# Attention of a sixth pair in chunks of 64 tokens, a new order of steps, and 24 matmuls whose result nobody reads

## The chip, the cores and the metric

The kernel runs on one core of a Trainium2 chip. Its engines work side by side, each through its own list of instructions in order, and wait for one another by semaphores: TensorE (PE) multiplies, VectorE (DVE) and ScalarE (ACT) read PE's results from PSUM and do elementwise work, GpSimd (POOL) does elementwise work in SBUF, and SyncE (SP) issues most of the DMA transfers. The metric is the time of one execution on the device in microseconds (us); smaller is better. Before the change the median of six runs is 210.73 us (210.42 to 212.49).

## The reference

Two layers follow each other. The first is causal attention with a decay per head, written in blocks of 64 tokens with a running state; the second is layer norm, a two-layer MLP with ReLU, and a residual. Batch 4, 8 heads, 768 tokens, head size 64, model width 512, hidden width 2048.

```python
for b in range(nb):                       # blocks of 64 tokens
    intra = (qb @ kb.T * Dmask) @ vb      # Dmask[i, j] = lam ** (i - j) for i >= j
    inter = (qb * lam_pow) @ kv_state
    out[:, :, sl] = intra + inter
    kv_state = lam_block * kv_state + (kb * rev_pow).T @ vb
x = out, heads side by side               # 4 x 768 x 512
xn = (x - mean) / sqrt(var + 1e-6) * g_ln
result = x + relu(xn @ w_ch1) @ w_ch2
```

## The kernel before

The 4 x 768 tokens are cut into 12 windows of 256 tokens ("pairs" u = 0 to 11, a pair being two tiles of 128 tokens), four batches for each third of the sequence. The attention of a pair is computed by one of two methods. Pairs below `LB` (L60, six of them) use chunks of 128 tokens: two rounds of scores with 128 columns (`scores`, L273), four masks, and 64 small matmuls to apply them to the values (`av`, L419). Pairs from `LB` on use chunks of 64 tokens: one round of 32 scores matmuls with 64 columns (`scores64`, L353), two masks, and 32 matmuls (`av64`, L406), but a state after every chunk, so that VectorE makes two sums of 128x256 more (`Smid`, L388) and GpSimd two conversions more (`Sm`, L396). Each small matmul uses a quarter of the array and four run at once. `inter` (L432) adds what the state gives, `kv` (L307) or `kv64` (L372) makes the new state's terms.

The method also decides how the inputs are laid out. Below `LB`, `fill` (L76) loads k, q and v each with one transfer of 512 KB whose runs hold two tokens (512 bytes); from `LB` on (L80) with two transfers of 256 KB whose runs hold one token (256 bytes). `in_k_one`, `in_q_one` and `in_v` scale and convert a loaded pair to bf16 on the engine that the call names; `transpose_dma` (L257) transposes q (second argument 1) or k (0) by a DMA from SP's queue into `kqT`.

The MLP of a pair is a group g of 16 "units" of PE work. For groups 2 and 3, eight units of the first layer (`m1`, L530, 8 matmuls of 256 columns each, evicted by ScalarE at L533) and eight of the second (`m2`, L666, 4 matmuls of 512 columns). From group 4 on the second layer is computed with seven products instead of eight (`m2w`, L565), for which VectorE forms sums of weights (`w_sums`) and of hidden activations (`m2s[g].sums`).

The order of everything is written out by hand: a list of calls in which `units(n)` issues the next n units and the other calls issue attention steps, loads, conversions and transposes between them. The order in which calls stand is the order in every engine's list. Attention steps of pairs below `LB` stand alone (`s1`, `s2`, `s3`, `s4`); where the 64-token method begins, two pairs are interleaved by `X1` and `X2`, and from then on by `X`:

```python
def X1(u):                    def X2(u):
    av(u - 1, range(NP))          scores64(u)
    inter(u - 1, 0)               inter(u - 1, 1)
    kv64(u)                       mask64(u, 0)
    states64(u, 0)                norm(u - 1, 0)
    states64(u, 1)                norm(u - 1, 1)
                                  mask64(u, 1)
```

`X(u)` is the same in one piece. `inter` ends with `reader` (L443), a small copy from PSUM after which PE may write the second half into the same banks; up to pair 4 it runs on VectorE, later on ScalarE.

PSUM's eight banks carry names: `sc` (two), `po0`, `po1`, and `mm` (four), which `m1`, `m2`, `m2w`, `kv` and `kv64` take in turn. A bank is given again in the order in which its earlier holders are finished with in the list. `kin`, `qin`, `vin` and `kq` have three buffers each.

At the start, the norm weight arrives as one row and is spread over 128 partitions by a matmul with ones (`g_all`, L180, in the bank `po1`).

Of the kernel before, what the change touches and what calls it, by code (L numbers as in the profile page):

```python
# [7 lines left out]
F32 = mybir.dt.float32  # L8
# [9 lines left out]
def kernel(  # L18
# [11 lines left out]
    nc = tc.nc  # L30
# [26 lines left out]
    half = [slice(0, 64), slice(64, 128)]  # L57
    XB = 3
    X_PE = (2, 3, 4)
    LB = 6  # L60

    def mm_tile(shape, dtype, name):
        return ps.tile(shape, dtype, tag="mm", bufs=4, name=name)
# [29 lines left out]
    def load_in(u, name, eng):  # L93
        got = qkv_in[u][name]
        fill(got, name, u, slice(0, H), eng)
        qkv_in[u][name] = got.rearrange("p h (j d) -> p h j d", j=2)
# [28 lines left out]
    g_row = const.tile([128, DM], F32)  # L125
    g_one = wk.tile([1, DM], F32, tag="xc", name="g_one")
    nc.scalar.dma_start(g_one, moe_g_ln[None, :])


    ident = const.tile([128, 128], BF16)  # L130
# [20 lines left out]
    def make_keep64():  # L151
        for dst, base in ((keep64, 0), (keep64_b, D)):
            nc.gpsimd.memset(dst, 1.0)
            nc.gpsimd.affine_select(
                out=dst, in_=dst, compare_op=ALU.is_ge, fill=0.0,
                base=base, pattern=[[1, D]], channel_multiplier=-1,
            )
        nc.vector.tensor_copy(keep64[half[1]], keep64_b[half[1]])
# [18 lines left out]
    ones = const.tile([1, 128], F32)  # L177
    nc.vector.memset(ones, 1.0)
    g_all = ps.tile([128, DM], F32, tag="po1", name="g_all")
    nc.tensor.matmul(g_all, lhsT=ones, rhs=g_one, start=True, stop=True)  # L180

    lnlam = const.tile([128, H], F32)
# [15 lines left out]
    def open_window(u):  # L198
        kq = wk.tile([128, 2, NP, 2, 2, D], BF16, tag="kq", bufs=3, name="kq")
        vb = wk.tile([128, H, 2, D], BF16, tag="vb", bufs=4, name="vb")  # L200
        st[u] = dict(kq=kq, vb=vb)
        if u < XB:
            st[u]["kqT"] = wk.tile([128, 2, NP, 2, 128], BF16, tag="kqT", bufs=3, name="kqT")
# [25 lines left out]
    def in_k_one(u, eng, j):  # L229
        src = qkv_in[u]["k"].rearrange("p (a e) j d -> p a e j d", e=2)  # L230
        (eng.copy if eng is nc.scalar else eng.tensor_copy)(part(0, st[u]["kq"], ALL)[:, :, :, j], src[:, :, :, j])

    def in_q_one(u, eng, j):
        src = qkv_in[u]["q"].rearrange("p (a e) j d -> p a e j d", e=2)
        lq = (lam_q[:, :, j] if u < LB else lam_p[:, 0, :]).rearrange("p (a e) -> p a e", e=2)
        eng.tensor_tensor(part(1, st[u]["kq"], ALL)[:, :, :, j], src[:, :, :, j],  # L236
                          lq[:, :, :, None].to_broadcast([128, NP, 2, D]), op=ALU.mult)

    def in_v(u, eng, hs=ALL):
        n = hs.stop - hs.start  # L240
        lv = lam_v[:, hs, :, None] if u < LB else lam_p[:, 1, hs, None, None]
        eng.tensor_tensor(st[u]["vb"][:, hs], qkv_in[u]["v"][:, hs], lv.to_broadcast([128, n, 2, D]), op=ALU.mult)  # L242
# [453 lines left out]
    def store(u):  # L696
        for j in range(2):
            nc.sync.dma_start(rows_of(u)[j], o_of[u][half[j]])
# [82 lines left out]
    def w_sums(c, n):  # L781
        v = w2[c].rearrange("p (k e) d -> p k e d", e=2)
        w = DM // 2
        b11, b12, b21, b22 = v[:, :, 0, 0:w], v[:, :, 0, w:], v[:, :, 1, 0:w], v[:, :, 1, w:]
        t1, t2, t3, t4 = (wt[c][:, :, i] for i in range(4))
        if n == 0:
            nc.vector.tensor_tensor(t1, b12, b11, op=ALU.subtract)
            nc.vector.tensor_tensor(t3, b12, b22, op=ALU.add)
        else:
            nc.vector.tensor_tensor(t2, b11, t3, op=ALU.subtract)  # L790
            nc.vector.tensor_tensor(t4, t2, b21, op=ALU.add)
# [28 lines left out]
    def s1(u):  # L820
        kv(u)
        scores(u, 0)
        new_state(u, 0, nc.gpsimd)
        mask(u, 0, (0,))
        new_state(u, 1, nc.gpsimd)
        mask(u, 0, (1,))
# [38 lines left out]
    def s2(u):  # L865
        scores(u, 1)
        mask(u, 1)

    def s3(u):
        av(u, range(NP))  # L870
        inter(u, 0)
        if st[u]["S"][0][1] is None:
            norm(u, 0)
# [5 lines left out]
    def s4(u):  # L879
        inter(u, 1)  # L880
        if st[u]["S"][0][1] is not None:
            norm(u, 0)
        norm(u, 1)
# [144 lines left out]
    def units(n):  # L1028
        for _ in range(n):
            f, *a = next(steps)  # L1030
            f(*a)
# [40 lines left out]
    in_q_one(4, nc.gpsimd, 0)  # L1072
    in_q_one(4, nc.gpsimd, 1)
    in_v(4, nc.gpsimd)
    units(5)
    w_sums(0, 0)
    w_sums(0, 1)
    units(2)
    w_sums(1, 0)
    units(1)  # L1080
    s1(3)
    store(0)
    transpose_dma(4, 0)
    transpose_dma(4, 1)
    units(2)
    s2(3)
    units(1)
    open_window(5)
    in_k_one(5, nc.gpsimd, 0)
    in_k_one(5, nc.gpsimd, 1)  # L1090
    in_q_one(5, nc.gpsimd, 0)
    in_q_one(5, nc.gpsimd, 1)
    in_v(5, nc.gpsimd)
    units(1)
    s3(3)
    units(1)
    s4(3)
    open_in(6, False)
    load_in(6, "k", nc.sync)
    units(1)  # L1100
    load_in(6, "q", nc.sync)
    units(1)
    w_sums(1, 1)
    load_in(6, "v", nc.sync)
    units(1)
    w_sums(2, 0)
    transpose_dma(5, 0)
    units(1)
    make_keep64()
    to_xT(3, 0)  # L1110
    transpose_dma(5, 1)
    open_in(7, False)
    load_in(7, "k", nc.sync)
    units(1)
    w_sums(2, 1)
    s1(4)
    to_xT(3, 1)
    open_window(6)
    in_k_one(6, nc.scalar, 0)
    units(1)  # L1120
    rstd_of(3)
    in_k_one(6, nc.gpsimd, 1)
    units(2)
    open_window(7)
    s2(4)
    units(2)
    s3(4)
    units(1)
    in_q_one(6, nc.vector, 1)
    in_v(6, nc.gpsimd)  # L1130
    s4(4)
    in_q_one(6, nc.vector, 0)
    units(3)
    load_in(7, "q", nc.sync)
    units(1)
    w_sums(3, 0)
    w_sums(3, 1)
    units(1)
    open_in(8, False)
    to_xT(4, 0)  # L1140
    units(1)
    to_xT(4, 1)
    s1(5)
    units(1)
    transpose_dma(6, 1)
    units(1)
    in_q_one(7, nc.gpsimd, 0)
    units(1)
    in_q_one(7, nc.gpsimd, 1)
    s2(5)  # L1150
    transpose_dma(6, 0)
    units(2)
    rstd_of(4)
    units(1)
    X1(6)
    in_k_one(7, nc.vector, 1)
    load_in(7, "v", nc.sync)
    load_in(8, "k", nc.sync)
    in_v(7, nc.gpsimd)
    units(1)  # L1160
    in_k_one(7, nc.scalar, 0)
    units(1)
    X2(6)
    open_window(8)
    units(3)
    m2s[4].sums(0, 4)
    units(1)
    store(1)
    store(2)
    to_xT(5, 0)  # L1170
    transpose_dma(7, 0)
    transpose_dma(7, 1)
    units(1)
    open_in(9, False)
    units(1)
    in_k_one(8, nc.gpsimd, 0)
    units(1)
    m2s[4].sums(4, 8)
    units(1)
    to_xT(5, 1)  # L1180
    units(1)
    in_k_one(8, nc.vector, 1)
    units(2)
    load_in(8, "q", nc.sync)
    load_in(8, "v", nc.sync)
    units(2)
    rstd_of(5)
    X(7)
    units(1)
    in_q_one(8, nc.gpsimd, 0)  # L1190
    in_q_one(8, nc.gpsimd, 1)
    load_in(9, "k", nc.sync)
    units(1)
    in_v(8, nc.gpsimd)
    units(1)
    to_xT(6, 0)
    transpose_dma(8, 1)
    transpose_dma(8, 0)
    to_xT(6, 1)
    load_in(9, "q", nc.sync)  # L1200
    load_in(9, "v", nc.sync)
    open_in(10, False)
    load_in(10, "k", nc.sync)
    units(3)
    m2s[5].sums(0, 4)
    units(2)
    load_in(10, "v", nc.sync)
    units(2)
    open_window(9)
    units(1)  # L1210
    m2s[5].sums(4, 8)
    units(3)
    in_k_one(9, nc.scalar, 0)
    units(1)
    in_k_one(9, nc.scalar, 1)
    units(1)
    rstd_of(6)
    in_q_one(9, nc.gpsimd, 0)
    X(8)
    units(1)  # L1220
    in_q_one(9, nc.gpsimd, 1)
    open_window(10)
    units(3)
    open_in(11, False)
    units(1)
    to_xT(7, 0)
    units(1)
    transpose_dma(9, 1)
    transpose_dma(9, 0)
    to_xT(7, 1)  # L1230
    units(2)
    store(3)
    units(2)
    m2s[6].sums(0, 4)
    m2s[6].sums(4, 8)
    units(3)
    store(4)
    load_in(10, "q", nc.sync)
    units(3)
    rstd_of(7)  # L1240
    units(1)
    in_v(9, nc.gpsimd)
    in_k_one(10, nc.gpsimd, 1)
    in_k_one(10, nc.gpsimd, 0)
    X(9)
    in_v(10, nc.gpsimd)
    in_q_one(10, nc.gpsimd, 0)
    units(1)
    transpose_dma(10, 0)
    units(1)  # L1250
    in_q_one(10, nc.vector, 1)
    units(1)
    to_xT(8, 0)
    units(2)
    to_xT(8, 1)
    units(1)
    transpose_dma(10, 1)
# [99 lines left out]
```

## Time and profile before

| | us |
|---|---|
| median of six runs | 210.73 |
| the profiled execution: its own time | 210.88 |
| its span, first to last instruction | 209.2 |
| PE busy in the span | 198.9 |
| VectorE, ScalarE, GpSimd busy | 139.1, 119.1, 86.3 |

The profiled execution's span is 1.7 us shorter than its time; that much lies around it. Shares over the whole span hide the stages, so here are stretches of it, each with the busy time of every engine:

| stretch, us | PE | VectorE | ScalarE | GpSimd | DMA, GB/s |
|---|---|---|---|---|---|
| 40 to 60 | 20.00 | 12.73 | 7.12 | 9.89 | 252 |
| 60 to 80 | 20.00 | 14.19 | 12.01 | 9.96 | 213 |
| 80 to 100 | 20.00 | 14.30 | 11.70 | 8.06 | 179 |
| 100 to 120 | 19.98 | 16.61 | 12.85 | 9.38 | 174 |
| 120 to 140 | 20.00 | 14.07 | 13.17 | 10.65 | 198 |
| 140 to 160 | 20.00 | 15.85 | 12.84 | 8.92 | 161 |
| 160 to 180 | 20.00 | 13.93 | 12.97 | 3.59 | 34 |
| 180 to 200 | 20.00 | 11.46 | 10.36 | 1.51 | 146 |

A matmul's end is modelled in such a profile and overlaps with the next one's start, so "busy" does not yet say that PE runs at its best rate; for that the distance between the starts of neighbouring matmuls has to be read. PE's first matmul starts at 4.18 us [...].

### The profile page before, as it was taken

The numbers are of one execution on the slowest core, as the hardware profiler recorded it, in microseconds if no ns is written. First come the engines' busy times: TensorE is split into PE (matmuls) and PEld (weight loads), VectorE is DVE, ScalarE is ACT, GpSimd is POOL, SyncE is SP. The second block draws the span as 40 slices with busy tenths as digits, with TensorE's granted clock in tenths as the row PEclk, the third lists the DMA queues.
The fourth block names the chain that finished last, engine by engine and source line by source line (L and its number), as shares of the span: only waits on it lengthen the run. The fifth ranks groups of instructions, "written<-read, shape, count | busy, mean of one in ns | idle before, by whom it ended". The sixth has DMA issues, their size and how long they took to land.

```text
span 209.2 us, 7231 instructions
## 1 busy us (share of the span) xinstructions
PE 198.9 (95%) x3099; PEld 156.6 (75%) x3099; DVE 139.1 (67%) x277; ACT 119.1 (57%) x275; POOL 86.3 (41%) x118
## 2 busy tenths in 40 slices
PE   2989999999999999999999999999999999999992
PEld 0469788544685587478888888888888888888881
DVE  2587580439675776757898776667877947865263
ACT  3834869326254667347566675585596565652620
POOL 4679137319647330626265441782274202011020
PEclk9999999999999999999999999999999999999998
DMA  4999999999899999995899999895988020158403
GB/s 108 298 269 216 193 292 181 183 308 278 149 321 187 219 167 211 169 296 55 179 180 156 188 211 168 197 202 107 229 134 189 3 50 3 24 127 279 129 18 82
DMA packets 91041, 36.38 MB, mean 174 GB/s; under 512 B 65153, under 2 KB 88193, under 8 KB 91010
## 3 DMA queue, kind: packets, MB, share of 16 engines
q1 hardware_dynamic: 86400, 31.53, 72.5%
q0 software_dynamic: 4224, 4.19, 12.8%
q8 instruction: 24, 0.39, 0.8%
q10 hardware_dynamic: 386, 0.20, 0.4%
q14 instruction: 7, 0.06, 0.1%
HBM read 27.27 MB, written 6.29 MB: 160 GB/s over the span
## 4 chain that ended last, share of the span: by engine, by line
PE 73%; DMA 11%; issue 7%; POOL 3%; SPq 2%; DVE 1%; POOLq 0%; ACT 0%; ACTq 0%; DVEq 0%
PE pm L530 32%; PE pm L666 14%; PE pwa L565 6%; PE pwd L565 5%; PE pwc L565 5%; DMA w<-in_moe_w_ch_dram 4%; DMA qin<-in_q_dram 4%; DMA kin<-in_k_dram 3%; PE pwb L565 3%; SPq L76 2%; PE po L432 1%; PE po L419 1%; PE sc L273 1%; DVE x L578 1%; PE po L406 1%
## 5 line engine op out<-in xcount | busy, mean ns | idle before, releaser
L530 PE MATMUL pm<-xT,w 128*128 128x256 bf16 x736 | 84.9, 273 | 0.0
L530 PEld LDWEIGHTS <-w 128*128 128x128 bf16 x736 | 70.4, 98 | 9.7 <-DVE Smid L388 0.3
L533 ACT ACTIVATE hT<-pm 128x512 f16<-128x512 f32 x92 | 54.1, 598 | 29.2 <-PE pm L530 29.1
L666 PE MATMUL pm<-w,hT 128*128 128x512 f16 x128 | 30.2, 380 | 0.0
L565 PEld LDWEIGHTS <-hs 128*128 128x128 f16 x256 | 24.9, 98 | 2.9
L313 POOL TENSOR_TENSOR Sn<-Stmp,lam_s 128x256 bf16<-128x256 f32 x16 | 9.8, 616 | 38.0 <-DVE Stmp L317 20.1
L590 POOL TENSOR_TENSOR x<-ev_u,x 128x256 f32<-128x256 f32 x8 | 6.5, 817 | 45.0 <-ACT ev_u L589 45.0
L548 DVE TENSOR_TENSOR hs<-hT 128x1024 f16<-128x1024 f16 x16 | 12.8, 797 | 16.0 <-ACT hT L533 16.0
L565 PEld LDWEIGHTS <-hT 128*128 128x128 f16 x192 | 18.1, 98 | 3.6 <-ACT hT L533 1.6
L666 PEld LDWEIGHTS <-hT 128*128 128x128 f16 x128 | 11.6, 98 | 12.1
L283 DVE TENSOR_TENSOR mA<-sc,keep 128x512 bf16<-128x512 f32 x20 | 13.1, 683 | 7.1 <-PE sc L273 7.1
L458 ACT ACTIVATE x<-po 128x512 f32<-128x512 f32 x18 | 10.6, 590 | 9.7 <-PE po L419 5.3
L460 DVE SCALAR_TENSOR_TENSOR xc<-po,nmean,g_row 128x512 bf16<-128x512 f32 x18 | 13.0, 745 | 3.6 <-ACT nmean L459 3.6
L242 POOL TENSOR_TENSOR vb<-vin,lam_p 128x1024 bf16<-128x1024 f32 x6 | 11.6, 1935 | 3.8 <-DMA vin<-in_v_dram 3.8
L503 ACT ACTIVATE sq<-x,nmean 128x512 bf16<-128x512 f32 x18 | 12.9, 719 | 0.3
L578 DVE SCALAR_TENSOR_TENSOR x<-pwd,rstd,x 128x256 f32<-128x256 f32 x16 | 7.7, 482 | 7.8 <-POOL x L598 7.8
L236 POOL TENSOR_TENSOR kq<-qin,lam_q 128x512 bf16<-128x512 f32 x10 | 10.3, 1048 | 5.9 <-PE po L432 3.1
L242 POOL TENSOR_TENSOR vb<-vin,lam_v 128x1024 bf16<-128x1024 f32 (+1 forms) x7 | 11.8, 1688 | 1.0 <-ACT kqT L251 1.0
L494 ACT COPY xT<-xt 128x512 bf16<-128x512 bf16 x10 | 5.8, 583 | 9.0 <-PE xt L493 9.0
L550 DVE TENSOR_TENSOR hs<-hs,hT 128x512 f16<-128x512 f16 x16 | 10.1, 628 | 0.6
L236 POOL TENSOR_TENSOR kq<-qin,lam_p 128x512 bf16<-128x512 f32 x9 | 9.3, 1045 | 2.4 <-PE po L432 2.0
L578 DVE SCALAR_TENSOR_TENSOR x<-pwa,rstd,x 128x512 f32<-128x512 f32 (+1 forms) x16 | 9.1, 613 | 0.8
(128 smaller groups left out, 303.3 us busy)
## 6 DMA issues: line engine op xcount, KB each, us to landing
out_dram<-x SPq DMA_DIRECT2D x22, 256.0 KB, 4.0
w<-in_moe_w_ch_dram POOLq DMA_DIRECT2D x8, 512.0 KB, 8.8
kin<-in_k_dram SPq DMA_DIRECT2D x14, 256.0 KB, 5.1
qin<-in_q_dram SPq DMA_DIRECT2D x14, 256.0 KB, 4.5
vin<-in_v_dram SPq DMA_DIRECT2D x14, 256.0 KB, 5.3
kin<-in_k_dram SPq DMA_DIRECT2D x5, 512.0 KB, 6.8
qin<-in_q_dram SPq DMA_DIRECT2D x5, 512.0 KB, 8.6
vin<-in_v_dram SPq DMA_DIRECT2D x5, 512.0 KB, 8.5
```

The source lines that it names most:

```text
L236: eng.tensor_tensor(part(1, st[u]["kq"], ALL)[:, :, :, j], src[:, :, :, j], lq[:, :, :, None].to_broadcast([128, NP, 2, D]), op=ALU.mult)
L242: eng.tensor_tensor(st[u]["vb"][:, hs], qkv_in[u]["v"][:, hs], lv.to_broadcast([128, n, 2, D]), op=ALU.mult)
L283: nc.vector.tensor_tensor(s[f"mA{hf}"][:, e], s[f"sc{hf}"][e], kp[:, None, :, :].to_broadcast([128, 2, 2, 128]), op=ALU.mult)
L458: nc.scalar.activation(x, po, ACT.Copy, accum_out=sm)
L460: nc.vector.scalar_tensor_tensor(xc, in0=po, scalar=nm, in1=g_row, op0=ALU.add, op1=ALU.mult)
L503: nc.scalar.activation(sq, s["x"][:, ab], ACT.Square, bias=s["nmean"][:, ab:ab + 1], accum_out=ss[:, ab:ab + 1])
L530: nc.tensor.matmul(pm[:, b, :], lhsT=w1[n // W2K][:, kk, (n % W2K) * 128:(n % W2K + 1) * 128], rhs=xT_of[g][:, kk, 0:N], start=(b == 0 and ...
L533: nc.scalar.activation(hT[:, u * NB:(u + 1) * NB, 0:N], pm, ACT.Relu)
L548: nc.vector.tensor_tensor(s13, b[:, :, 1:2, :].to_broadcast([128, n, 2, 128]), b[:, :, 0:4:3, :], op=ALU.subtract)
L565: nc.tensor.matmul(pr[bank], lhsT=lhs(r), rhs=rhs, start=(first and r == 0), stop=(r == KB // 2 - 1), skip_group_check=True)
L578: nc.vector.scalar_tensor_tensor(out, in0=in0, scalar=r[ab], in1=in1, op0=ALU.mult, op1=ALU.add)
L666: nc.tensor.matmul(acc[i], lhsT=hT[:, kk, i * 128:(i + 1) * 128], rhs=w2[kk // W2K][:, kk % W2K, :], start=(kk == 0), stop=(kk == KB - 1))
```

## The change

`LB` goes from 6 to 5. Pair 5, the sixth, is thereby computed in chunks of 64 tokens, loaded in runs of 256 bytes, and stored in the other row order; it needs no step `s1`, `s2` of its own, since `X1(5)`, `X2(5)` and `X(6)` take the place of `s3(4)`, `s4(4)`, `s1(5)`, `s2(5)`, `X1(6)` and `X2(6)`. The list of steps is written anew from the second layer of group 1 (unit 18) to the middle of group 7. Many conversions go from GpSimd to VectorE or ScalarE. At the start, 24 matmuls of 8 columns are put ahead of `g_all`, on a tile of zeros that VectorE fills first; they write a corner of the bank `po0`, which nobody reads.

```diff
-    LB = 6
+    LB = 5
...
+    fill_in = const.tile([128, 8], BF16)
+    nc.vector.memset(fill_in, 0.0)
...
     g_all = ps.tile([128, DM], F32, tag="po1", name="g_all")
+    fill_ps = ps.tile([128, 8], F32, tag="po0", name="idle")
+    for _ in range(24):
+        nc.tensor.matmul(fill_ps[0:8], lhsT=fill_in, rhs=fill_in, start=True, stop=True)
     nc.tensor.matmul(g_all, lhsT=ones, rhs=g_one, start=True, stop=True)
```

Of the list, the part from pair 4's conversions to `X` of pair 6, with several calls on one line; the number is that of the units issued before:

```diff
-23 w_sums(0, 0); w_sums(0, 1)   25 w_sums(1, 0)
-26 s1(3); store(0); transpose_dma(4, 0); transpose_dma(4, 1)   28 s2(3)
-29 open_window(5); in_k_one(5, gpsimd, 0 and 1); in_q_one(5, gpsimd, 0 and 1); in_v(5, gpsimd)
-30 s3(3)   31 s4(3); load_in(6, "k")   32 load_in(6, "q")   33 w_sums(1, 1); load_in(6, "v")
-34 w_sums(2, 0); transpose_dma(5, 0)   35 make_keep64(); to_xT(3, 0); transpose_dma(5, 1); load_in(7, "k")
-36 w_sums(2, 1); s1(4); to_xT(3, 1); in_k_one(6, scalar, 0)   37 rstd_of(3); in_k_one(6, gpsimd, 1)
-39 s2(4)   41 s3(4)   42 in_q_one(6, vector, 1); in_v(6, gpsimd); s4(4); in_q_one(6, vector, 0)
-45 load_in(7, "q")   46 w_sums(3, 0); w_sums(3, 1)   47 to_xT(4, 0)   48 to_xT(4, 1); s1(5)
-49 transpose_dma(6, 1)   50 in_q_one(7, gpsimd, 0)   51 in_q_one(7, gpsimd, 1); s2(5); transpose_dma(6, 0)
-53 rstd_of(4)   54 X1(6); in_k_one(7, vector, 1); load_in(7, "v"); load_in(8, "k"); in_v(7, gpsimd)
-55 in_k_one(7, scalar, 0)   56 X2(6)
+20 transpose_dma(4, 1)   21 transpose_dma(4, 0)   22 open_window(5); in_q_one(5, gpsimd, 0)
+23 w_sums(1, 0)   24 w_sums(0, 0); w_sums(0, 1)   26 s1(3); in_k_one(5, gpsimd, 0)
+28 w_sums(1, 1)   29 s2(3)   31 in_q_one(5, vector, 1); load_in(6, "k"); s3(3); transpose_dma(5, 1)
+32 load_in(6, "q"); s4(3)   33 load_in(6, "v"); make_keep64(); in_k_one(5, scalar, 1)
+35 w_sums(2, 0); w_sums(2, 1)   36 in_v(5, gpsimd); s1(4); to_xT(3, 0); transpose_dma(5, 0)
+37 to_xT(3, 1)   38 in_k_one(6, gpsimd, 1)   39 in_k_one(6, gpsimd, 0); s2(4); rstd_of(3)
+40 in_q_one(6, vector, 1)   41 w_sums(3, 0)   42 X1(5)
+45 transpose_dma(6, 0); load_in(7, "k"); store(0); in_q_one(6, gpsimd, 0)   47 w_sums(3, 1)
+48 in_v(6, gpsimd)   49 X2(5); load_in(7, "q")   51 rstd_of(4); to_xT(4, 0); in_q_one(7, gpsimd, 1)
+52 to_xT(4, 1)   53 in_q_one(7, vector, 0); load_in(7, "v"); transpose_dma(6, 1)
+54 in_k_one(7, scalar, 0); in_v(7, vector)   55 in_k_one(7, scalar, 1)   57 X(6)
```

Units 22 to 29 and 38 to 45 are the first layers of groups 2 and 3, 30 to 37 and 46 to 53 their second layers; group 4 begins at unit 54. After that `X(7)` stays at unit 69, `X(8)` goes from 85 to 86, `X(9)` stays at 102 and `X(10)` at 118. Conversions of pairs 8, 9 and 10 are dealt out anew among GpSimd, VectorE and ScalarE, and the loads of v of pairs 8 and 9 and of q of pair 10 are issued at other places.

More of the change, by code (lines that the diff above doesn't have):

```diff
@@ L1074 @@
     in_v(4, nc.gpsimd)
-    units(5)
+    units(2)
+    transpose_dma(4, 1)
+    units(1)
+    transpose_dma(4, 0)
+    units(1)
+    open_window(5)
+    in_q_one(5, nc.gpsimd, 0)
+    units(1)
+    w_sums(1, 0)
+    units(1)
     w_sums(0, 0)
@@ L1078 @@
     units(2)
-    w_sums(1, 0)
+    s1(3)
+    in_k_one(5, nc.gpsimd, 0)
+    units(2)
+    w_sums(1, 1)
     units(1)
[L1081 to L1084, printed above, removed]
+    s2(3)
     units(2)
[L1086 to L1097, printed above, removed]
+    in_q_one(5, nc.vector, 1)
     open_in(6, False)
@@ L1099 @@
     load_in(6, "k", nc.sync)
+    s3(3)
+    transpose_dma(5, 1)
     units(1)
     load_in(6, "q", nc.sync)
+    s4(3)
     units(1)
-    w_sums(1, 1)
     load_in(6, "v", nc.sync)
+    make_keep64()
+    in_k_one(5, nc.scalar, 1)
+    units(2)
+    open_in(7, False)
+    w_sums(2, 0)
+    open_window(6)
+    w_sums(2, 1)
     units(1)
-    w_sums(2, 0)
+    in_v(5, nc.gpsimd)
+    s1(4)
+    to_xT(3, 0)
     transpose_dma(5, 0)
     units(1)
-    make_keep64()
-    to_xT(3, 0)
-    transpose_dma(5, 1)
@@ L1112 @@
-    open_in(7, False)
-    load_in(7, "k", nc.sync)
-    units(1)
[L1115 to L1119, printed above, removed]
+    to_xT(3, 1)
+    units(1)
+    in_k_one(6, nc.gpsimd, 1)
     units(1)
+    in_k_one(6, nc.gpsimd, 0)
+    s2(4)
     rstd_of(3)
-    in_k_one(6, nc.gpsimd, 1)
-    units(2)
     open_window(7)
-    s2(4)
-    units(2)
-    s3(4)
     units(1)
     in_q_one(6, nc.vector, 1)
-    in_v(6, nc.gpsimd)
-    s4(4)
-    in_q_one(6, nc.vector, 0)
@@ L1133 @@
-    units(3)
-    load_in(7, "q", nc.sync)
     units(1)
     w_sums(3, 0)
+    units(1)
+    X1(5)
+    units(3)
+    transpose_dma(6, 0)
+    load_in(7, "k", nc.sync)
+    store(0)
+    in_q_one(6, nc.gpsimd, 0)
+    units(2)
+    open_in(8, False)
     w_sums(3, 1)
     units(1)
-    open_in(8, False)
+    in_v(6, nc.gpsimd)
+    units(1)
+    X2(5)
+    load_in(7, "q", nc.sync)
+    units(2)
+    rstd_of(4)
     to_xT(4, 0)
+    in_q_one(7, nc.gpsimd, 1)
     units(1)
     to_xT(4, 1)
-    s1(5)
@@ L1144 @@
     units(1)
+    in_q_one(7, nc.vector, 0)
+    load_in(7, "v", nc.sync)
     transpose_dma(6, 1)
     units(1)
-    in_q_one(7, nc.gpsimd, 0)
+    in_k_one(7, nc.scalar, 0)
+    in_v(7, nc.vector)
     units(1)
[L1149 to L1153, printed above, removed]
-    units(1)
[L1155 to L1159, printed above, removed]
+    in_k_one(7, nc.scalar, 1)
+    units(1)
+    open_window(8)
@@ L1160 @@
     units(1)
[L1161 to L1164, printed above, removed]
+    X(6)
     units(3)
-    m2s[4].sums(0, 4)
-    units(1)
     store(1)
     store(2)
+    load_in(8, "k", nc.sync)
+    units(1)
     to_xT(5, 0)
-    transpose_dma(7, 0)
     transpose_dma(7, 1)
-    units(1)
     open_in(9, False)
     units(1)
+    m2s[4].sums(0, 4)
+    transpose_dma(7, 0)
+    m2s[4].sums(4, 8)
+    units(2)
+    to_xT(5, 1)
+    units(3)
+    in_k_one(8, nc.scalar, 1)
+    load_in(8, "q", nc.sync)
@@ L1176 @@
+    units(1)
+    rstd_of(5)
+    units(1)
+    X(7)
+    units(1)
+    in_q_one(8, nc.gpsimd, 1)
+    load_in(8, "v", nc.sync)
     in_k_one(8, nc.gpsimd, 0)
     units(1)
[L1178 to L1191, printed above, removed]
     load_in(9, "k", nc.sync)
-    units(1)
@@ L1194 @@
     in_v(8, nc.gpsimd)
+    in_q_one(8, nc.vector, 0)
     units(1)
@@ L1197 @@
     transpose_dma(8, 1)
+    to_xT(6, 1)
     transpose_dma(8, 0)
-    to_xT(6, 1)
     load_in(9, "q", nc.sync)
-    load_in(9, "v", nc.sync)
     open_in(10, False)
     load_in(10, "k", nc.sync)
-    units(3)
+    units(5)
     m2s[5].sums(0, 4)
+    units(1)
+    m2s[5].sums(4, 8)
+    units(1)
+    open_window(9)
+    units(2)
+    in_k_one(9, nc.gpsimd, 0)
+    units(2)
+    in_k_one(9, nc.scalar, 1)
+    transpose_dma(9, 0)
+    load_in(9, "v", nc.sync)
     units(2)
     load_in(10, "v", nc.sync)
[L1208 to L1215, printed above, removed]
     units(1)
     rstd_of(6)
-    in_q_one(9, nc.gpsimd, 0)
     X(8)
+    open_window(10)
+    in_q_one(9, nc.gpsimd, 1)
+    in_k_one(10, nc.scalar, 0)
     units(1)
-    in_q_one(9, nc.gpsimd, 1)
-    open_window(10)
-    units(3)
+    in_q_one(9, nc.vector, 0)
+    to_xT(7, 0)
+    units(2)
+    transpose_dma(9, 1)
     open_in(11, False)
+    units(2)
+    to_xT(7, 1)
+    m2s[6].sums(0, 4)
     units(1)
-    to_xT(7, 0)
+    load_in(10, "q", nc.sync)
     units(1)
[L1228 to L1231, printed above, removed]
     store(3)
     units(2)
-    m2s[6].sums(0, 4)
+    store(4)
     m2s[6].sums(4, 8)
     units(3)
-    store(4)
-    load_in(10, "q", nc.sync)
+    rstd_of(7)
+    units(4)
+    in_v(9, nc.gpsimd)
+    X(9)
+    in_q_one(10, nc.vector, 1)
+    in_v(10, nc.gpsimd)
     units(3)
-    rstd_of(7)
+    in_k_one(10, nc.scalar, 1)
     units(1)
[L1242 to L1247, printed above, removed]
-    units(1)
[L1249 to L1254, printed above, removed]
+    in_q_one(10, nc.vector, 0)
+    transpose_dma(10, 0)
+    to_xT(8, 0)
+    units(1)
     to_xT(8, 1)
```

## The prediction

> **What bounds the kernel now.** I read the page's busy times first, then the stretches by engine (PE is busy for all of every 20 us between 40 and 200), then PE's order of time, to see whether a busy PE is also a full one. From the page:
>
> ```profile
> PE 198.9 (95%) x3099; PEld 156.6 (75%) x3099; DVE 139.1 (67%) x277; ACT 119.1 (57%) x275; POOL 86.3 (41%) x118
> ```
>
> PE's instructions in order of time, from the end of pair 4's attention to the first pair in 64-token chunks (start, duration, line, tiles, shape, count):
>
> ```profile
> 75.30 0.77 PE L419 MATMUL po<-vb,mA 64*64 64x64 bf16 x64
> 75.90 0.30 PE L432 MATMUL po<-Sn,kqT 64*64 64x64 bf16 x16
> 76.14 1.05 PE L530 MATMUL pm<-xT,w 128*128 128x256 bf16 x8
> 77.11 0.32 PE L432 MATMUL po<-Sn,kqT 64*64 64x64 bf16 x16
> 77.36 3.67 PE L530 MATMUL pm<-xT,w 128*128 128x256 bf16 x32
> ...
> 83.13 0.45 PE L307 MATMUL pk<-vb,kq 64*64 64x64 bf16 x32
> 83.41 0.40 PE L273 MATMUL sc<-kqT 64*64 64x128 bf16 x16
> 83.74 2.76 PE L666 MATMUL pm<-w,hT 128*128 128x512 f16 x12
> 86.43 0.42 PE L273 MATMUL sc<-kqT 64*64 64x128 bf16 x16
> 86.78 2.76 PE L666 MATMUL pm<-w,hT 128*128 128x512 f16 x12
> 89.47 0.71 PE L419 MATMUL po<-vb,mA 64*64 64x64 bf16 x64
> ...
> 90.66 1.92 PE L530 MATMUL pm<-xT,w 128*128 128x256 bf16 x16
> 92.51 0.45 PE L353 MATMUL sc<-kqT 64*64 64x64 bf16 x32
> 92.79 0.30 PE L432 MATMUL po<-Sn,kqT 64*64 64x64 bf16 x16
> 93.02 5.52 PE L530 MATMUL pm<-xT,w 128*128 128x256 bf16 x48
> ```
>
> No row carries a wait. Twelve matmuls of 512 columns from 86.78 start 0.216 us apart, so the next could start at 89.37; the attention piece delays it to 90.66 and costs 1.29. Going through all matmul starts of the trace from 35 to 205 us like this, only one place between MLP matmuls is more than 0.12 us late: 0.19 at 106.75. PE is full, and the time falls only if PE gets less to do.
>
> That place counts below, because it shows a PSUM bank being waited for. The row of weight loads names the releaser, and VectorE's order of time shows its chain after `X1(6)`:
>
> ```profile
> L530 PEld LDWEIGHTS <-w 128*128 128x128 bf16 x736 | 70.4, 98 | 9.7 <-DVE Smid L388 0.3
> ```
>
> ```profile
> 90.81 0.42 DVE L388 TENSOR_TENSOR Smid<-pk,Sn 128x256 f32<-128x256 f32 x1 [0.48 <-PE pk L372]
> 91.34 0.42 DVE L391 TENSOR_TENSOR Stmp<-pk,Smid 128x256 f32<-128x256 f32 x1
> 92.56 0.42 DVE L388 TENSOR_TENSOR Smid<-pk,Sn 128x256 f32<-128x256 f32 x1 [0.79 <-POOL Sn L313]
> ```
>
> The second `Smid` waits for GpSimd's new state, and only at its end (92.98) is the bank of `pk0` free: 2.32 us after PE resumed at 90.66.
>
> [...] a score matmul lasts 311 ns between 9 and 10 us and 216 to 222 after 20. [...] here a 512-byte packet took 31 ns in the mean and a 256-byte one 24, so the bytes cost about 1.5 times as much in halves. [...] the q conversion on VectorE took 1.94 us at 76.42 beside GpSimd's v conversion, and 0.68 at 80.14 alone.
>
> **The change part by part.**
>
> *PE's work.* The cost of a piece is the delay that it puts between MLP matmuls, as above. Removed: `s3(4)` 0.93, `s4(4)` 0.34, `s1(5)` 0.70 (0.92 with the 0.22 of four transposes that stay), `s2(5)` 0.44, `X1(6)` 1.28, `X2(6)` 0.60; sum 4.29. Added: `X1(5)`, which issues the same matmuls as `X1(6)`, 1.28; `X2(5)` 0.60; `X(6)`, like `X(7)`, for which the product at 103.72 resumes at 105.21, less 0.11 for one matmul, 1.38; sum 3.26. Gain 1.03 us, certain as far as PE stays full. Some 0.3 of it are three fewer switches between MLP and attention, at 0.1 each.
>
> *The bank behind X1(5).* `X1(6)` was followed by two units and then by `X2(6)`; the third unit came at 93.02, when the bank was just free (92.98). `X1(5)` is followed by three units at once. Banks go round in order: after `X1` two `mm` banks are free for the first two units and the third takes `pk0`'s. It wants to start two units of 0.9, that is 1.80 us, after PE resumes; the bank is free at 2.32 plus 0.06 for the signal. I take a wait of 0.5; at most 1.0, if VectorE is late (ahead of `Smid` stand two sums of weights, 0.42 each, and pair 4's `reader`), at least 0, if the banks come in another order.
>
> *X(6) and X(8)* also come directly before first-layer units. At `X(9)`, which already stands so, PE resumes at 135.46, the second `Smid` ends at 137.20, and the third unit is due at 137.27; I take 0.05 in all, up to 0.3 if VectorE's v conversion of pair 7 (some 1.4, twice the 0.68 of half the elements) is still running.
>
> *to_xT(4, 0)* now comes two units of 0.864 after `X2(5)`: 1.73. Its input needs ScalarE's copy, mean, and VectorE's product; after `s4(3)`, where PE resumed at 64.92, that ended at 66.74, 1.82 later. Wait 0.1; `rstd_of(4)` then holds ScalarE for 1.9 ahead of the two copies of xT, which end about 4.7 after `X2(5)`, while group 4 starts at 4.9: no wait, 0.4 if ScalarE slips.
>
> *Loads of pair 5.* They are issued from 54.75 as before, now as six transfers. In the trace the three landed at 59.4, 61.2 and 62.8; later 256 KB transfers landed about 1.2 apart, so now k at 60.5, q at 62 to 63, v at 65. GpSimd waits for q ahead of pair 3's last state and the k half; neither is needed before `X(7)` and `X1(5)`. VectorE's q half stands ahead of pair 3's `reader`, which `s4(3)` needs at 65.4: the masks of `s2(3)` end about 63.4, the conversion 0.7 later, so there is 1 us left. SP goes on with both transposes of pair 4, now ahead of `store(0)`: landing about 68.5 (67.8 before), needed by `s1(4)` at 69.4. Cost 0, and the cover is 0.9 us.
>
> *The other moves.* `store(0)` and pair 7's loads go behind pair 5's and 6's transposes on SP; nobody waits for that store before pair 6's norm takes its buffer in `X(7)`. Pair 6's transposes end near 88, needed at 91; pair 7's near 102.5, needed at 104; pair 8's over 2 us ahead. k of pair 10 comes earlier, since v of pair 9 no longer stands before it, and ScalarE's conversion finds it landed. `rstd_of(3)` ahead of three evictions was also done before without a wait. `w_sums` run in VectorE's idle time. The two extra `Smid` and `Sm` of pair 5 and its two masks fewer lie beside PE. Nothing.
>
> *The 24 matmuls.* PE waits until 4.18 for the weight's row; at under 0.1 us each the 24 fit into the 3 us before. Should they bring the full clock sooner, PE reaches 34.46 sooner and waits there longer for GpSimd's q of pair 2, whose load landed at 32.6: today PE waits 0.25 there, so no more than that is to be had. I take 0.
>
> Sum: -1.03 + 0.5 + 0.05 + 0.1 = -0.4. From the profiled execution's own 210.88 (span 209.2 and 1.7 around it) this gives 210.5; that execution lay 0.15 above the median, so 210.4 against 210.73.
>
> **The rivals.**
>
> *The bank wait doesn't come* (banks in another order, or three units slow enough). For it: it rests on an order that I infer from one wait of 0.19. Against: that wait was for just this instruction. Then -0.9, 209.9.
>
> *The transfers of pair 5 come late: slower.* If a 256-byte packet took as long as one of 512, the three inputs would land 3.4 apart from 59.4 plus 1.7: 61.1, 64.5, 67.9, and pair 4's transposes at about 71.5 instead of 67.8; `s1(4)` would wait some 2 us at 69.4, with `s4(3)` waiting 0.3 inside of it. It decides from a landing of those transposes after 69.4, and makes the kernel slower than before from 69.8. For it: DMA is near full between 40 and 80 us. Against: the 24 ns per packet. Then -0.4 + 2.0, 212.3.
>
> *The 24 matmuls bring the clock earlier*: 0.25 more, 210.1, and 209.6 together with the first. [...]
>
> **How the numbers follow.** About 0.5%, 1.05 us, is what a measurement of this kernel can tell from no change. My forecast 0.45, its own range 209.9 to 210.9; no bank wait 0.23 (209.5 to 210.2); late transfers or another wait of that size 0.22 (211.0 to 212.8); earlier clock 0.10 (209.5 to 210.3). Below 209.68 lie a third of the second and fourth case and a little of the first: 0.15. Above 211.78 lie most of the third: 0.18. The range of 209.5 to 212.1 leaves about 0.1 on either side.
>
> **What would show it.** Right: 32 matmuls of L273 and 32 of the values' fewer on PE's list, pieces of about 1.3, 0.6 and 1.4 us at `X1(5)`, `X2(5)` and `X(6)`, a gap of about 0.5 before the third unit after `X1(5)` put down to `Smid`, none at `s1(4)` and `s4(3)`. Wrong: a PE gap put down to `reader` or to pair 4's transposes, a gap over 0.3 at `to_xT(4)` or group 4's first unit, or a full clock long before 20 us with a time that falls by more than 0.3 for it.

## The result and the profile after

The changed kernel's median is 212.1 us (211.1 to 213.39, 29 runs), that of the kernel before on the same chips 210.74 (210.16 to 212.72, 64 runs). The ratio is 1.0052, with a 95% interval of 1.0038 to 1.0067: about 1.1 us slower (the medians alone lie 1.4 apart), where 0.3 us faster was forecast. The profiled executions differ by 1.4 us: 212.26 against 210.88, spans of 210.6 and 209.2.

From the page of the changed kernel, the engines' row and the queues that carry instructions (packets, MB, share of the engines' time):

```profile
PE 198.8 (94%) x3091; PEld 156.4 (74%) x3091; DVE 141.7 (67%) x281; ACT 120.3 (57%) x278; POOL 81.0 (38%) x114
...
q8 instruction: 24, 0.39, 0.8%
...
q14 instruction: 8, 0.07, 0.1%
```

PE has eight matmuls fewer in all (32 fewer, 24 unread ones more), and is busy as long as before in a span 1.4 us longer. Where the span grew is read by following the same unit of MLP work through both traces. Each row is the change of one stretch against the profile of the kernel before, in us; the later columns are experiments told of below.

| stretch, in the kernel before | after | after again | without the 24 matmuls | fastest version | fastest with the 24 |
|---|---|---|---|---|---|
| start to 35.17 | +0.63 | +0.47 | +0.27 | +1.66 | +0.37 |
| to the unit directly behind `X(6)` in after (93.91) | -0.92 | -0.86 | -0.83 | -0.92 | -1.06 |
| the next three units (to 96.63) | +0.67 | +0.74 | +0.06 | +0.05 | +0.47 |
| to 132.47 | -0.10 | -0.01 | -0.09 | +0.05 | +0.14 |
| one product of group 6 (to 133.23) | +0.64 | +0.64 | +0.64 | 0.00 | 0.00 |
| to the last product (204.12) | -0.10 | 0.00 | +0.10 | +0.12 | -0.13 |
| the tail, to the end of the span | +0.56 | +0.68 | +0.56 | +0.01 | +0.07 |
| sum | +1.38 | +1.66 | +0.71 | +0.97 | -0.14 |

The forecast gain is there, in the second row. Three losses at fixed places eat it; what is lost before 35 us comes on top and scatters between executions (see the last experiment). The first is behind `X(6)`. PE in order of time, in the changed kernel:

```profile
92.34 0.45 PE L411 MATMUL po<-vb,mA 64*64 64x64 bf16 x32
92.74 0.47 PE L377 MATMUL pk<-vb,kq 64*64 64x64 bf16 x32
93.03 0.50 PE L358 MATMUL sc<-kqT 64*64 64x64 bf16 x32
93.62 2.40 PE L535 MATMUL pm<-xT,w 128*128 128x256 bf16 x19
96.46 1.81 PE L535 MATMUL pm<-xT,w 128*128 128x256 bf16 x15 [0.44 <-issue]
```

19 matmuls are two units and three matmuls: PE stands in the middle of the third unit, and the bracket names no engine but "issue". The last two starts lie 0.71 us apart (95.75 and 96.46) instead of 0.11, so the stand costs 0.60. At the start of that unit, behind the matmul at 95.26, a short wait of 0.15 for the bank of `pk0` stands too.

The second loss is a product of group 6. VectorE and PE in order of time, first before, then after:

```profile
132.07 0.48 DVE L578 SCALAR_TENSOR_TENSOR x<-pwd,rstd,x 128x256 f32<-128x256 f32 x1 [1.05 <-POOL x L598]
...
133.12 1.04 PE L565 MATMUL pwd<-w,hs 128*128 128x256 f16 x8
...
134.11 0.15 DVE L508 RECIPROCAL rstd<-std 128x2 f32<-128x2 f32 x1
```

```profile
133.42 0.17 DVE L513 RECIPROCAL rstd<-std 128x2 f32<-128x2 f32 x1 [2.12 <-ACT std L509]
133.51 0.48 DVE L583 SCALAR_TENSOR_TENSOR x<-pwd,rstd,x 128x256 f32<-128x256 f32 x1
...
134.04 1.03 PE L570 MATMUL pwd<-w,hs 128*128 128x256 f16 x8 [0.48 <-DVE x L583]
```

`rstd_of(7)` moved from behind unit 101 to behind unit 98. Its reciprocal now stands in VectorE's list ahead of the eviction that frees the bank `pwd`, and waits there 2.12 us for ScalarE's square root. The next product into `pwd` starts 0.64 us late.

The third loss is at the very end. The transfers of the last microseconds (206 to 208.9 us: packets of each queue), before and after:

```profile
q10 hardware_dynamic: 195, 0.15, 21.6%
q1 hardware_dynamic: 160, 0.13, 19.0%
```

```profile
q1 hardware_dynamic: 240, 0.20, 29.3%
q10 hardware_dynamic: 240, 0.20, 28.1%
q14 instruction: 1, 0.01, 1.5%
```

Among the last stores an 8 KB packet of instructions is fetched (207.75 to 208.45 us). In the kernel before it comes at 209.5 us, behind everything. From the end of VectorE's last eviction to the end of the span it is 3.59 us before and 4.16 after.

### The profile page after: what moved, and what is told of

It reads as the page before. It is cut to its first block, busy times and chain, and to the rows that moved or that the text cites. A ratio compares the mean times of both kernels' runs of the same rounds, so it can differ in the third digit from the quotient of the medians.

```text
span 210.6 us, 7227 instructions
## 1 busy us (share of the span) xinstructions
PE 198.8 (94%) x3091; PEld 156.4 (74%) x3091; DVE 141.7 (67%) x281; ACT 120.3 (57%) x278; POOL 81.0 (38%) x114
## 4 chain that ended last, share of the span: by engine, by line
PE 67%; DMA 13%; issue 7%; DVE 4%; POOL 3%; SPq 3%; ACT 1%; POOLq 0%; DVEq 0%; ACTq 0%
PE pm L535 29%; PE pm L671 13%; PE pwa L570 5%; PE pwd L570 5%; DMA w<-in_moe_w_ch_dram 5%; PE pwc L570 5%; DMA qin<-in_q_dram 4%; DMA kin<-in_k_dram 3%; PE pwb L570 2%; SPq L76 2%; DMA out_dram<-x 1%; PE po L437 1%; DVE x L583 1%; PE po L411 1%; PE sc L358 1%
## 5 line engine op out<-in xcount | busy, mean ns | idle before, releaser
L288 DVE TENSOR_TENSOR mA<-sc,keep 128x512 bf16<-128x512 f32 x16 | 10.4, 683 | 6.8 <-PE sc L278 6.8
L555 DVE TENSOR_TENSOR hs<-hs,hT 128x512 f16<-128x512 f16 x16 | 11.6, 727 | 0.5
L364 DVE TENSOR_TENSOR mA<-sc,keep 128x512 bf16<-128x512 f32 x14 | 9.5, 679 | 2.9 <-PE sc L358 2.9
L241 POOL TENSOR_TENSOR kq<-qin,lam_q 128x512 bf16<-128x512 f32 x8 | 8.2, 1044 | 7.4 <-DMA qin<-in_q_dram 7.4
L247 POOL TENSOR_TENSOR vb<-vin,lam_v 128x1024 bf16<-128x1024 f32 (+1 forms) x6 | 9.7, 1621 | 1.7 <-DMA vin<-in_v_dram 1.4
L241 POOL TENSOR_TENSOR kq<-qin,lam_p 128x512 bf16<-128x512 f32 x7 | 7.2, 1041 | 7.6 <-DMA qin<-in_q_dram 4.3
```

What stands on the lines that cost most here:

```text
L288: nc.vector.tensor_tensor(s[f"mA{hf}"][:, e], s[f"sc{hf}"][e], kp[:, None, :, :].to_broadcast([128, 2, 2, 128]), op=ALU.mult)
L555: nc.vector.tensor_tensor(s4, s2, b[:, :, 2], op=ALU.add)
```

## The experiments

All ratios are against the kernel before on the same chip, with the 95% interval. The expectations call "unit 19" the first-layer unit that starts at 35.17 us in the trace of the kernel before, and count matmuls from 0; their "fourth unit behind `X(6)`" is the third. Their P3 is the product of group 6 that starts late, and P5 the one whose eviction it waits for. The "tail" is the time from VectorE's last eviction to the end of the span.

**The changed kernel once more**, nothing edited.

> The changed kernel unaltered, once more. Theory 1, fixed costs: the wait of 0.64 us at the product P3 behind the reciprocal of rstd_of(7) at 133 us, the stand of 0.60 us inside the fourth unit behind X(6) at 96 us and the lag of 0.63 us by unit 19 recur within 0.1 us, and the time is 1.0045 to 1.006 of before. Theory 2, scatter of one execution: the stand at 96 us and the lag at the start differ by more than 0.3 us; only the wait at P3, which has its cause in the order of DVE's list, recurs.

Measured: 1.0078 (1.0051 to 1.0105). The wait of 0.64 at group 6 and the stand behind `X(6)` recur, the latter after exactly the same number of matmuls (1502 recorded ones before it; 0.78 between the starts). The lag at the start is 0.47 instead of 0.63, so it differs by more than the 0.1 of theory 1; the wait and the stand are no accidents of one execution.

**`rstd_of(7)` back by three units.**

```diff
     units(3)
-    rstd_of(7)
-    units(4)
+    units(3)
+    rstd_of(7)
+    units(1)
     in_v(9, nc.gpsimd)
```

> The changed kernel with rstd_of(7) put back three units, directly ahead of the unit before X(9). Theory 1: P5's eviction no longer stands behind a reciprocal that waits for ACT's square root, the wait of 0.64 us at P3 goes, the units from 102 on come 0.6 us earlier and the ratio falls by 0.003, to about 1.002. Rival: the wait only moves, because the eviction or P3 has another wait next, or the tail takes the gain: ratio stays at 1.005.

Measured: 1.0010 (0.9989 to 1.0030). VectorE in this kernel:

```profile
132.79 0.48 DVE L583 SCALAR_TENSOR_TENSOR x<-pwd,rstd,x 128x256 f32<-128x256 f32 x1 [1.05 <-POOL x L603]
133.38 1.14 DVE L583 SCALAR_TENSOR_TENSOR x<-pwa,rstd,x 128x512 f32<-128x512 f32 x2
...
134.83 0.16 DVE L513 RECIPROCAL rstd<-std 128x2 f32<-128x2 f32 x1
```

The eviction is ahead of the reciprocal again and the step of 0.64 at that product is gone. Theory 1 holds for the wait. The stand behind `X(6)` was longer in this execution, 1.56 between the two starts, again after 1502 matmuls.

**The changed kernel without the 24 matmuls** (with their tile and its fill).

```diff
-    fill_in = const.tile([128, 8], BF16)
-    nc.vector.memset(fill_in, 0.0)
...
-    for _ in range(24):
-        nc.tensor.matmul(fill_ps[0:8], lhsT=fill_in, rhs=fill_in, start=True, stop=True)
```

> The changed kernel without the 24 unread matmuls and their tile. Theory 1: they cost nothing and bring nothing, the lag of 0.63 us by unit 19 stays, ratio 1.005. Rival a: the lag comes from them (they hold the norm weight's spread back, and with it ACT's and DVE's first work): lag gone, ratio 1.002. Rival b: they bring the full clock forward: without them the first 20 us are longer, ratio above 1.006.

Measured: 1.0008 (0.9990 to 1.0026). My theory 1 was wrong: the matmuls cost something, and in the profile more of it at the stand behind `X(6)`, which has gone (0.61 us in that row of the table), than at the start (0.36). Rival b did not come: a 128x128 matmul of PE lasts some 310 ns just ahead and 219 or 220 from 20.85 us on in the changed kernel, from 20.17 on in the kernel before, and without the 24 the score matmuls from 20.71 on are as fast as those from 20.65 on in the kernel before (16 in 0.42 us). The granted clock reads 1.00 in every stretch from 0 to 24 us of all three. PE in order of time:

```profile
93.35 4.37 PE L530 MATMUL pm<-xT,w 128*128 128x256 bf16 x37
```

**The kernel before with the 24 matmuls alone** (the same lines added).

> The kernel before with the 24 unread matmuls alone. Theory 1: unit 19 starts within 0.15 us of before, ratio 0.9995 to 1.0005. Rival a: lag of 0.6 us by unit 19, ratio 1.003. Rival b: earlier full clock, ratio 0.998.

Measured: 1.0162 (1.0137 to 1.0186), 3.4 us on the medians, more than any expectation. The profile loses 1.40 before 35 us, 1.53 up to the first of two stands and with it, and 0.67 at the second. PE in order of time at the first:

```profile
94.20 0.27 PE L437 MATMUL po<-Sn,kqT 64*64 64x64 bf16 x11
95.78 0.24 PE L437 MATMUL po<-Sn,kqT 64*64 64x64 bf16 x5 [1.31 <-issue]
```

This is other work, in the middle of `X2(6)`, yet there are 1502 matmuls before it again. A second stand (0.78 between starts) comes after 1757 matmuls. That points to the mechanism: 255 matmuls with their weight loads are 510 instructions. The page counts 24 packets of 16 KB in q8 for PE's 6182 recorded instructions, 258 a packet (254, counted from the start of the second packet to that of the last), so 510 are about two packets. From this I take that PE stands where a packet of its own program begins, until that packet has come by DMA. In the trace's packet records it landed at 94.87, 94.81, 95.53 and 94.29 us in after, after again, the second experiment and this one, and PE went on 1.59, 1.62, 1.36 and 1.49 us later. By this account the 24 matmuls are not costly there themselves: they move every later packet boundary 24 matmuls to an earlier point of the work. At one of these points an `X` lies just ahead, which runs through 128 small matmuls in 1.3 us (in the changed kernel, from 92.34 on, the first four start within 0.01 us and the next four 0.05 later).

**Both edits together**: no unread matmuls, `rstd_of(7)` back.

> The changed kernel without the 24 unread matmuls and with rstd_of(7) back, both edits together. Theory: the two add up; the profile shows no stand behind X(6) and no wait at P3 at 133 us, the last unit starts 0.5 us ahead of that of the kernel before, the tail behind it keeps its extra 0.55 us, ratio 0.998 to 1.000. Rival: the gains overlap (what one brings the other takes), ratio above 1.001.

Measured: 1.0016 (0.9990 to 1.0041); medians 210.74 and 210.71. It is inconclusive as a time: the runs scatter from 210.0 to 213.0. The profiled one took 213.0 and lost over 2 us at 13 to 16 us, waiting for a load of k. Behind 35 us it shows what was expected: no stand, no wait at group 6, 0.95 us gained from there to the last product. The tail keeps its extra 0.6 (4.24). Since either edit alone gave 1.0010 and 1.0008, the times do not show that the two gains add; only the stretches of the profile do.

**Fewer instructions on ScalarE**: as the last, and four conversions of k taken off ScalarE (ACT). With waits and DMA issues the trace then has 319 records of ScalarE, where the changed kernel has 325 and the kernel before 321.

```diff
-    in_k_one(7, nc.scalar, 1)    in_k_one(8, nc.scalar, 1)
+    in_k_one(7, nc.vector, 1)    in_k_one(8, nc.vector, 1)
-    in_k_one(10, nc.scalar, 0)   in_k_one(10, nc.scalar, 1)
+    in_k_one(10, nc.gpsimd, 0)   in_k_one(10, nc.gpsimd, 1)
```

> As the last, and four readers (pair 7 and 8, second half of k, to DVE; pair 10, both halves of k, to POOL) are taken off ACT, so that ACT runs as many instructions as in the kernel before. Theory 1: ACT's own instruction packet of 8 KB no longer comes at 207 us, beside the last stores, but behind the end as in the kernel before; the span ends 3.5 us behind the last DVE eviction instead of 4.1, ratio 0.0025 lower than the last. Rival: the extra 0.55 us at the end belongs to the order of the last steps; it stays, ratio as the last.

Measured: 1.0063 (1.0038 to 1.0088), a miss as a time, though theory 1 holds for the tail: it is 3.63 us and the instruction packet comes at 210.5. What took it back is my choice of readers. ScalarE and PE in order of time:

```profile
153.82 0.62 ACT L231 CAST kq<-kin 128x512 bf16<-128x512 f32 x1 [1.07 <-DMA kin<-in_k_dram]
...
159.47 0.61 PE L565 MATMUL pwc<-wt,hs 128*128 128x256 f16 x4 [0.93 <-DVE hs L548]
```

The conversion of pair 11's second half of k waits for its load, so ScalarE's ReLUs behind it run late and PE loses 1.1 us at 158. The expectation of the next such kernel blames the buffer that pair 10's readers free later. The traces show something else: SyncE's transpose of pair 10's k waits for the conversion that I moved to GpSimd:

```profile
138.34 1.07 POOL L231 CAST kq<-kin 128x512 bf16<-128x512 f32 x1
...
139.44 1.25 SPq L257 DMA_TRANSPOSE kqT<-kq  x1
```

Against PE's work this transpose starts 1.05 us later than without this edit (140.81 there, in an execution that by then runs 2.42 us later). What stands behind it on SyncE's list comes later too: the last transfer of pair 11's k is issued 0.7 us later against PE's work. It also takes 6.0 us to land instead of 4.2, and why isn't settled.

**48 unread matmuls instead of 24.**

```diff
-    for _ in range(24):
+    for _ in range(48):
```

> The changed kernel with 48 unread matmuls in place of 24. Theory 1, PE's instructions: PE stands again at the 1502nd matmul of its program, where a packet of its instructions begins, now 24 matmuls earlier in the work (in the first unit behind X(6)), and goes on about 1.5 us behind the landing of the packet; it stands 1.2 to 2.5 us instead of 0.6 to 1.6, ratio above 1.008. Rival: the stand belongs to the fourth unit behind X(6) (its bank, or the stores issued there) and stays in that unit at 0.6 to 0.8 us, ratio as the changed kernel.

Measured: 1.0067 (1.0047 to 1.0088). Both expectations missed: there is no stand at all.

```profile
93.99 3.71 PE L535 MATMUL pm<-xT,w 128*128 128x256 bf16 x31
```

I had taken the lateness as depending on `X(6)` alone. Here the packet landed at 91.90 us, before `X(6)` started at 92.65; in after it landed at 94.87, 2.5 us behind the start of `X(6)`. It started at 90.92, when the first of the stores of pairs 1 and 2 had only just been issued (SP issues them from 89.5 us on). So position and DMA traffic seem to decide together, which the next two runs test. The time did not fall with the stand: against after, the profile loses 0.19 before 35 us, 0.26 at 65 us and 0.13 in the tail.

**The stores of pairs 1 and 2 and the load of pair 8's k later**, by four units (the expectation says six).

```diff
     units(3)
-    store(1)
-    store(2)
-    load_in(8, "k", nc.sync)
     units(1)
...
     units(2)
+    store(1)
+    store(2)
+    load_in(8, "k", nc.sync)
     to_xT(5, 1)
```

> The changed kernel with the stores of pairs 1 and 2 and the load of k of pair 8 issued six units later. Theory 1a: the packet of PE's instructions waits behind nothing of these; the stand of 0.6 to 0.8 us at the 1502nd matmul stays. Theory 1b: their 0.6 MB hold the packet up; it lands 0.5 us or more earlier and the stand falls below 0.3 us, ratio 0.003 lower than the changed kernel.

Measured: 1.0509 (1.0481 to 1.0538). The packet landed at 93.25 and the stand is gone, as theory 1b says. The time is another matter: the conversion of that k is called only three units behind the load's new place.

```profile
109.58 0.62 ACT L236 CAST kq<-kin 128x512 bf16<-128x512 f32 x1 [8.35 <-DMA kin<-in_k_dram]
```

It waits 8.35 us for the load and PE waits for `reader` behind it, 7.6 us at 112. I had not followed the load to its reader.

**The two stores alone, later**, by five units (the expectation says eight steps).

```diff
     units(3)
-    store(1)
-    store(2)
     load_in(8, "k", nc.sync)
...
     to_xT(5, 1)
-    units(3)
+    units(1)
+    store(1)
+    store(2)
+    units(2)
```

> The changed kernel with the stores of pairs 1 and 2 alone issued eight steps later; the load of k of pair 8 stays. Theory 1b: the packet of PE's instructions that landed at 94.8 us lands at 93.3 us, no stand at the 1502nd matmul, ratio 0.003 below the changed kernel (1.002 of before). Rival: the stand returns or moves to a load that the later stores now hold up, ratio 1.005 or more.

Measured: 1.0215 (1.0176 to 1.0255). The same DMA view, from 91.9 to 93.7 us, first of the changed kernel, then of this one:

```profile
DMA packets 272, 0.50 MB, mean 275 GB/s; under 512 B 30, under 2 KB 30, under 8 KB 272
```

```profile
DMA packets 1, 0.02 MB, mean 9 GB/s; under 512 B 0, under 2 KB 0, under 8 KB 0
...
q8 instruction: 1, 0.02, 3.3%
```

In the changed kernel 272 packets move and the instruction packet has not begun; here it is the only packet. Of the 272, 242 are of 2 KB, as the stores write them, and none of the 256 bytes in which k is loaded. The instruction packet starts 0.12 us behind the start of `X(6)` instead of 1.65, lands at 93.65, and PE doesn't stand. So the packet waits behind the stores. The time is worse all the same, since the stores now hold later loads up: a conversion of k waits 2.35 us at 126, and starts of PE lie 1.25 apart at 119 and 2.03 at 127. The rival is right as to the time.

**Other conversions off ScalarE.** Without the 24 matmuls, `rstd_of(7)` back, and:

```diff
-    in_k_one(5, nc.scalar, 1)   in_k_one(9, nc.scalar, 1)
+    in_k_one(5, nc.gpsimd, 1)   in_k_one(9, nc.gpsimd, 1)
-    in_k_one(7, nc.scalar, 1)   in_k_one(8, nc.scalar, 1)
+    in_k_one(7, nc.vector, 1)   in_k_one(8, nc.vector, 1)
```

> As the kernel without the matmuls and with rstd_of(7) back, and four readers off ACT again, this time others: the second half of k of pairs 5 and 9 to POOL, of pairs 7 and 8 to DVE; those of pair 10 stay on ACT, so that the load of k of pair 11 gets its buffer as early as before. Theory: the tail is that of the kernel before (3.5 us from the last DVE eviction to the end of the span), the wait at 158 us is gone, ratio 0.995 to 0.9975. Rival: one of the moved readers comes late on its new engine and takes it back, ratio above 0.999.

Measured: 209.96 against 210.97 us, ratio 0.9952 (0.9934 to 0.9969). This beats both kernels. From its page, and PE behind `X(6)`:

```profile
q14 instruction: 7, 0.06, 0.1%
```

```profile
94.65 4.69 PE L530 MATMUL pm<-xT,w 128*128 128x256 bf16 x40
```

Seven packets on q14 in the span, a tail of 3.61 us, no stand, no wait at 133 or 158. Its profiled execution, at 211.84 the slowest of 22, lost 1.66 us before 35 us; from there on it gains 0.69 on the kernel before.

**Four idle ScalarE instructions in the kernel before.**

```diff
     m2s[6].sums(4, 8)
-    units(3)
+    units(1)
+    nc.scalar.activation(sqrt_first, eps_t, ACT.Sqrt)
...
     store(4)
```

(four times, one behind each of four units)

> The kernel before with four more ACT instructions of one number a partition (a square root whose result nobody reads), one behind each of four units near 120 us, so that ACT's program has as many instructions as that of the changed kernel. Theory 1: ACT's last instruction packet comes beside the last stores at about 207 us and the end of the span is 0.55 us later from the last eviction on, ratio 1.002 to 1.003. Rival: the tail of the changed kernel has another cause; the tail stays at 3.5 us, ratio 0.9995 to 1.001.

Measured: 1.0002 (0.9973 to 1.0030), which can't tell 0.5 us. The trace can. Among the transfers of 206 to 208.9 us:

```profile
q14 instruction: 1, 0.01, 1.4%
```

The packet comes at 206.9, the tail is 4.14 us, and the last product starts 0.08 us earlier than in the kernel before. Four instructions on the engine are enough to bring the extra 0.54, and since no other engine's list was changed, the packet is ScalarE's. ScalarE issues its last store 0.57 us behind VectorE's last eviction instead of 0.29, and it lands at 2.96 instead of 2.42. In all nine profiles with 325 records of ScalarE the packet starts when 322 of them have begun, and the tail is 4.00 to 4.29; in the five with 318 to 321 it comes behind the end, and the tail is 3.57 to 3.67.

**The fastest version with the 24 matmuls again.**

> The fastest kernel so far (rstd_of(7) back, four readers off ACT) with the 24 unread matmuls put in again. Theory: they cost what they cost in the changed kernel; PE stands at its 1502nd matmul behind X(6), q of pair 1 lands at about 17.1 us, and the ratio rises from 0.9952 to 0.998 to 1.001. Rival: the matmuls were harmless and the drop without them was scatter, ratio 0.994 to 0.9965.

Measured: 211.33 against 210.78 us, 1.0011 (0.9986 to 1.0036); without them the interval was 0.9934 to 0.9969. By the two ratios the 24 matmuls cost 0.0059 of 211, 1.2 us (0.6 to 1.9 by their intervals). PE in order of time:

```profile
95.86 1.37 PE L535 MATMUL pm<-xT,w 128*128 128x256 bf16 x11 [0.24 <-issue]
```

1502 matmuls lie before it again, its packet landed at 94.44, and the stand is 0.40 of the 1.2. A part of the rest may lie at the start. With 24 or 48 matmuls PE's first packet starts at 14.0 to 14.4 us in all eight profiles, in the middle of the load of pair 1's q, and GpSimd's conversion of it starts at 16.7 to 17.3; without them the packet starts at 15.0 to 15.7, and the conversion at 15.8 to 16.0 in four of six profiles. Without the matmuls, then with them:

```profile
15.92 2.05 POOL L236 TENSOR_TENSOR kq<-qin,lam_q 128x512 bf16<-128x512 f32 x2 [1.21 <-DMA qin<-in_q_dram]
```

```profile
17.17 2.05 POOL L241 TENSOR_TENSOR kq<-qin,lam_q 128x512 bf16<-128x512 f32 x2 [2.53 <-DMA qin<-in_q_dram]
```

That the packet holds the load up is argued from this coincidence; it wasn't isolated. PE's lag at 35 us scatters from -0.2 to +2.3 between executions without the matmuls and from -0.05 to +1.4 with them, so its share stays open.

## Why the prediction was wrong

- *PE's work, -1.03*: right. The pieces measure 1.29 (`X1(5)`), 0.60 (`X2(5)`) and 1.37 (`X(6)`) against 1.28, 0.60 and 1.38, and the stretch from 35 us to `X(6)` gains 0.92 in the profile and 0.86 in the repeat.
- *The bank behind X1(5), +0.5*: didn't come. 32 first-layer matmuls run through from 77.97 without a gap. The second `Smid` ends at 80.23, as late as the step had it (2.26 us after PE resumed, forecast 2.32), but it is the fourth unit, not the third, that waits for VectorE, and it comes at 80.60, when the bank is free. The order of banks was inferred from one wait; the first rival was right here.
- *X(6) and X(8) before first-layer units, +0.05*: `X(6)` costs 0.15 at the bank. Within its bound of 0.3.
- *to_xT(4, 0), +0.1*: the transposes cost 0.41 instead of their 0.22, a wait of 0.18.
- *Loads of pair 5, 0*: right. q landed at 62.8, v at 65.7, pair 4's transposes at 66.7 and 67.8, and PE waits for none of them. The slower rival, late transfers of pair 5, did not happen, though DMA was as full as the prediction says: eight or nine tenths in every slice of the page between 40 and 80 us, before and after.
- *The other moves, "Nothing"*: this step failed, twice. `rstd_of(7)` was not gone through at all, though VectorE's list says what it costs: a reciprocal that waits for ScalarE, ahead of an eviction that PE waits for, +0.64. And the moves make ScalarE's list longer by three conversions and a wait (325 records instead of 321), which brings its last instruction packet onto the last stores, +0.56 in the profile.
- *The 24 matmuls, 0*: this step failed. They were priced by their own time in an idle stretch, which is right: they take 0.74 us, and PE then waits 2.55 us for the norm weight. What the prediction calls the full clock is, in the records, the fall of a matmul's duration at about 20 us. The granted clock reads 1.00 before that fall too, the 24 matmuls did not bring it earlier (20.85 us against 20.17), and what brings it was not shown. That they displace all later instructions of PE in its stream was not seen: a stand of 0.60 in the profile and 0.4 to 1.5 over the runs, and perhaps some of the lag at the start. In the fastest version they cost 1.2 us in all.

The parts that were priced sum to -1.03 + 0 + 0.15 + 0.18 = -0.7, near the forecast of -0.4. The 1.4 us of the profile come from what wasn't: 0.64 + 0.56 + 0.60, and 0.63 at the start, whose cause stays open, less 0.35 that isn't accounted for.

## What to carry to other kernels

When steps of a hand-written order move, go through every one of them on the list of each engine on which it puts an instruction: here a reciprocal of 0.17 us waited 2.12 us for ScalarE and held up the eviction behind it, and a product started 0.64 us late. In this kernel, whose PE is busy for 94% of the span, 24 matmuls put in at the start came back as a stand of 0.60 us at the 1502nd matmul, and four idle instructions on ScalarE as 0.54 us at the end. So look for gaps marked "issue" that stay at the same count of instructions in different work, and for the DMA traffic just ahead of them: from 91.9 to 93.7 us 272 packets moved in the changed kernel, and the instruction packet alone once the two stores came later. Follow a store or load that is moved to relieve one place to its next buffer and reader: the stand of 0.60 went when pair 8's k was loaded four units later with the two stores, but the conversion of that k then waited 8.35 us and PE 7.6.

## What was unexpected of the hardware

As I read these traces, PE can stand until its own instructions have come. In the changed kernel's span 24 packets of 16 KB come in q8, one for 258 of PE's 6182 recorded instructions, and in the kernel before with the 24 matmuls PE stood behind 1502 and 1757 matmuls, 510 instructions or about two packets apart. Of the 24 packets in the changed kernel's span one goes with a stand of PE, and it costs 0.60. In five profiles PE stood 0.4 to 1.5 us at the same count, with a burst of small matmuls just ahead, and went on 1.36 to 1.62 us after the packet had landed; that the packet was late because of the stores is shown for the changed kernel. ScalarE's last packet is one of 8 KB, and among the last stores it lengthened the end by about 0.55 us (3.59 to 4.14 with four idle instructions added).
